# Four transfers and one group of products take another place in the order of a gated attention and ReGLU kernel (forward and gradients)

## The chip, the cores and the metric

The kernel runs on one core of one Trainium2 chip. The time is that of the device for one execution, in microseconds (us). Before the change the median of three runs is 909.66 us, from 908.64 to 911.75 us.

The core has five engines, each with its own queue of instructions that it takes in order: PE (TensorE, the matrix products), DVE (VectorE), ACT (ScalarE), POOL (GpSimd) and SP (SyncE, here used only to issue transfers). Transfers (DMAs) are issued from SP, from ACT and, for a few, from POOL.

## The reference

The kernel computes the output of a small network and all its gradients for one given gradient of the output. With S = 2048 tokens, D = 512, F = 1376, 32 heads of width 16 and a window of 256:

```
g   = sigmoid((x * gate_w).sum(-1))            # one gate per token
a   = attention(x @ wqkv, causal, window 256) @ wo     # O @ wo
b   = (relu(x @ W_gate) * (x @ W_up)) @ W_down # h @ W_down
out = g * a + (1 - g) * b
outputs: out, d/dx, d/dwqkv, d/dwo, d/dW_gate, d/dW_up, d/dW_down, d/dgate_w
```

All inputs and outputs are bf16. In the kernel, h is the inner product of the second branch, dg and du are the gradients of its two factors, O is the attention's output ahead of `wo`, and dq, dk, dv are the gradients of the attention's projections.

## The kernel before

The work has four stages. Every stage is written out by hand: the code emits each engine's instructions in the order in which they run.

**Stage 1, the second branch (lines 448 to 511, up to about 250 us).** A loop over n makes 44 steps: 11 blocks of 128 rows of F (`fc`) by 4 blocks of 512 tokens (`tg`). `at(lag)` is the step that began lag rounds earlier. In each round PE makes the gate product (`gate`, ACT then makes `rg`), the product `up` (DVE makes `upm`, POOL makes `hT`), the product `dh` of the step two rounds back (ACT makes `dh_sb`, DVE makes dg and POOL makes du, both in one tile `dgu`), and from round 6 on the weight gradients of the step six rounds back (`weights`, lines 402 to 436). The three products of the round share three PSUM buffers in turn (tag `mm`), so that the gate product of a round needs the buffer that ACT empties with `rg` of the round before. SP turns h and dg with du by transfers that transpose (`turn_h`, `turn_dgu`). ACT issues the stores of h, dg and du to scratch memory in HBM (`keep`, line 398): h of the step three rounds back, dg and du of the step four rounds back.

**Stage 2, the attention and its gradients (lines 512 to 974, about 250 to 705 us).** A loop over 360 units of 128 by 512 scores. Near its end, while the last units are still in work, it issues first loads for the next stage: `ev` holds actions for a later round, and line 897 puts the load of the first h (block 0, `load_h(0)`) two rounds behind unit row 13 and the second (`load_h(1)`) two rounds behind unit row 15. The stage spills its results (dq, dk, dv and O by rows) to the scratch `dqkvo_d`.

**Stage 3a, the first pass over the tokens (lines 976 to 1031, about 705 to 768 us).** Eight groups `g` of two blocks of 128 tokens. Before it starts, `load_a(0)` and `load_a(1)` load grad_out (`go_g`) and O (`o_t`) of groups 0 and 1; then come weights that are turned (`W_rest`), and the last of the gradients of `wqkv` (`S2["grads"]`, four products `wps` that DVE and ACT empty into `ws` in turn and that ACT stores). Per token block PE makes `bps` = h @ W_down (11 matmuls, ACT empties it into `b_all`) and adds four matmuls to `dwo` with `da_r`, which DVE makes from `go_g`.

**Stage 3b, the second pass (lines 1033 to 1110, about 768 us to the end).** The same groups. `load_b(g)` brings three operands: the rows of `dqkvo_d` turned by one transposing transfer (`T_g`, in the trace `turned`), `dgT_g` and `duT_g`. `load_b(0)` is issued in the first pass, ahead of block 12. Per block PE makes `aps` = O @ wo (4 matmuls, reads `T_g`), then `dx_in` (22 matmuls into `dxps`, from `dgT_g` and `duT_g`), then the part of the next block's sums `dgw` and `dx_qkv` (12 matmuls into `dxps`, reads `T_g`). From `aps` ACT, DVE and POOL make the output rows and the scalar `dz`, which `dx_out` needs to empty `dxps`.

**What else sets the order.** Each transfer that SP or ACT issues signals one of eight semaphores, taken in turn over both engines in the order of the program, and it waits until the transfer that had this semaphore before, eight issues earlier, has landed. While it waits, everything behind it on its engine waits too.

Of the kernel before, what the change touches and what calls it, by code (L numbers as in the profile page):

```python
# [12 lines left out]
F32 = mybir.dt.float32  # L13
# [9 lines left out]
def kernel(  # L23
# [20 lines left out]
    nc = tc.nc  # L44
    P = 128
# [4 lines left out]
    S, D = x_d.shape  # L50
# [7 lines left out]
    FC = (F + P - 1) // P  # L58
    TGW = min(512, S)
    NTG = S // TGW  # L60
    TPG = TGW // P
# [21 lines left out]
    dgT_d = dram.tile([F, S], BF, name="dgT_d")  # L83
    duT_d = dram.tile([F, S], BF, name="duT_d")
    dqkvo_d = dram.tile([S, 4 * D], BF, name="dqkvo_d")
# [112 lines left out]
    with ExitStack() as p1, tc.manual_schedule():  # L198
# [199 lines left out]
        def keep(k, *pairs):  # L398
            for dst, src in pairs:
                nc.scalar.dma_start(dst[k.fsl, k.ts], src)  # L400
# [47 lines left out]
        for n in range(N1 + 8):  # L448
            at = lambda lag: steps[n - lag] if 0 <= n - lag < N1 else None
            if at(0):  # L450
                gate(at(0))
                if 0 < n < NTG:
                    gate_col(n)
                if n == 2:
                    turn_wd0()
                if n + 1 < NTG:
                    turn_x(n + 1)
                if n == 0:
                    turn_gw()
                up(at(0))  # L460
                if n == 0:
                    gate_col(n)
                if n < NTG:
                    db_rows(n)
                if at(0).tg == 0 and at(0).fc > 0:
                    turn_wd(at(0).fc)
            if 1 <= n <= NTG:
                turn_db(n - 1)
            if at(2):
                dh(at(2))  # L470
            if at(1):
                turn_h(at(1))
            if at(3):
                keep(at(3), (hT_d, at(3).hT[:]))
            if at(4):
                turn_dgu(at(4))
                keep(at(4), (dgT_d, at(4).dgT), (duT_d, at(4).duT))
            if at(6):
                f = weights(at(6))
                if f is not None:  # L480
                    stores[n + 1] = f
            if n in stores:
                stores.pop(n)()
            t = n - DA0
            if t % 2 == 1 and 0 <= t // 2 < NT:
                make_da(t // 2)
            if t % 2 == 0 and 0 < t // 2 <= NT:
                turn_da(t // 2 - 1)
            if t == 2:
                nc.vector.reduce_sum(par[:, 0:1], par4[:], axis=AX.X)  # L490
                nc.vector.tensor_scalar(par[:, 1:2], par[:, 0:1], -1.0, 1.0, op0=ALU.mult, op1=ALU.add)
            if n == NTG + 1:
                nc.scalar.activation(tiny[:], tiny[:], ACT.Exp)
            if t in (NT + 3, 2 * NT + 1):
                i = (t - NT - 3) // (NT - 2)
                nc.gpsimd.memset(zt[i][:, 0, :, :, :], 0.0)
                nc.vector.memset(zt[i][:, 1, :, :, :], 0.0)
            if n == N1 - 2:
                first = project_parts(*groups[0])
            for _ in range({N1 + 1: 2, N1 + 2: 0}.get(n, 1)):  # L500
                if first:
                    first.pop(0)()
            if n == N1 + 2:
                second = project_parts(*groups[1])
            if n in (N1 + 2, N1 + 3, N1 + 4):
                second.pop(0)()
            z = n - DA0 - NT - 2
            if z == 0:
                load_w(0)
            if z % 4 == 3 and 0 < z // 4 + 1 < DC:  # L510
                load_w(z // 4 + 1)

    p3 = ctx
    if True:
# [55 lines left out]
        W6 = {}  # L570
# [91 lines left out]
        for c in range(DC):  # L662
            for j in range(NT):
                kbs = [k for k in (j - 1, j, j - 2) if k >= 0]
                for half in range(2):
                    order = kbs if half or len(kbs) < 3 else [kbs[0], kbs[2], kbs[1]]
                    for ki, kb in enumerate(order):
                        u = Unit()
# [129 lines left out]
        def load_f(dst, src_d, gsl):  # L798
            nc.sync.dma_start(dst[:, :nfull, :], src_d[0:nfull * P, gsl].rearrange("(fc p) s -> p fc s", p=P))
            if nfull < FC:  # L800
                nc.sync.dma_start(dst[:, nfull, :], src_d[F - P:F, gsl])

        def tokens(g):
            return slice(g * GT * P, (g + 1) * GT * P)

        def load_h(g):
            flat = wq.tile([P, 2, TPG, NP, P], BF, tag=f"z{g % 2}", name=f"h{g % 2}")[:].rearrange("p w t h q -> p (w t h q)")
            S2[f"h{g}"] = flat[:, 0:FC * GT * P].rearrange("p (c s) -> p c s", c=FC)
            load_f(S2[f"h{g}"], hT_d, tokens(g))
# [4 lines left out]
            return go_g  # L814

        def load_a(g):
            if g > 1:
                load_h(g)
            S2[f"go{g}"] = load_go(g)
            o_v = dqkvo_d[tokens(g), :].rearrange("(t p) (c a n) -> p t c a n", p=P, c=DC, a=4)  # L820
            for tl in range(GT):
                t = g * GT + tl
                o_t = pjA.tile([P, DC, P], BF, tag=("K0", "K1", "V0", "V1")[t % 4], name="o_t")
                nc.sync.dma_start(o_t[:], o_v[:, tl, :, 3, :])
                S2[f"o{t}"] = o_t

        def load_b(g):
            if g % 2 == 0:
                S2["T"] = st.tile([P, NT, 4, P], BF, tag="rows_st", name="turned")[:].rearrange("p t a n -> p (t a n)")
            n1 = 4 * DC * GT * P  # L830
            T_g = S2["T"][:, g % 2 * n1:(g % 2 + 1) * n1].rearrange("p (c s) -> p c s", c=4 * DC)
            nc.sync.dma_start_transpose(out=T_g, in_=dqkvo_d[tokens(g), :])
            dgT_g = S2["g6"].tile([P, FC, GT * P], BF, tag="dgT_g", name="dgT_g")
            load_f(dgT_g, dgT_d, tokens(g))
            duT_g = S2["g6"].tile([P, FC, GT * P], BF, tag="duT_g", name="duT_g")
            load_f(duT_g, duT_d, tokens(g))
            return T_g, dgT_g, duT_g

        with tc.manual_schedule():
            ev = {}  # L840
# [6 lines left out]
            n = 0  # L847
# [28 lines left out]
            while n <= NU + LAG or ev or cdq or bgq:  # L876
                now = ev.pop(n, [])
                u = units[n] if n < NU else None
                if u is not None:
                    gi = u.c * NTG + u.j // TPG  # L880
                    if u.first and u.j == 0:
                        sts[u.c] = st.tile([P, NT, 4, P], BF, tag="rows_st", name="rows_st")
                    if u.first and u.j % TPG == 0:
                        if gi + 1 < len(groups):
                            prq = project_parts(*groups[gi + 1]) if gi else second
                            due = n + sum(2 * min(3, j + 1) for j in range(u.j, u.j + TPG)) - 3
                            if gi + 2 == len(groups):
                                due -= 10
                    if u.first and u.j == TPG and ends:
                        copies.append(ends.pop(0))  # L890
                    if u.first and u.j == 1 and u.c > 0:
                        ready = grad_parts(u.c - 1)
                    if u.first and u.j == TPG - 1 and u.c > 0:
                        bgq += ready
                    front(u)
                    if u.last and gi + 1 == len(groups) and u.j % TPG in (1, 3):
                        ev.setdefault(n + 2, []).append(("dma", lambda i=(u.j % TPG) // 2: load_h(i)))
                for eng, f in now:
                    if eng == "pool":
                        f()  # L900
# [10 lines left out]
                w = units[n - LAG] if LAG <= n < NU + LAG else None  # L911
# [66 lines left out]
            S2["t6"] = ctx.enter_context(tc.tile_pool(name="t6", bufs=2))  # L978
            while late:
                late.pop(0)()  # L980
            load_a(0)
            load_a(1)
            for _ in range(4):
                W_rest.pop(0)()
# [7 lines left out]
    with ExitStack() as p56:  # L992
        x_r5 = x_r

        with ExitStack() as p6, tc.manual_schedule():
# [10 lines left out]
            for t in range(NT):  # L1006
                g, tl = t // GT, t % GT
# [25 lines left out]
            for g in range(NG):  # L1033
# [5 lines left out]
                for tl in range(GT):  # L1039
                    t = g * GT + tl  # L1040
                    tsl = slice(t * P, (t + 1) * P)
                    lsl = slice(tl * P, (tl + 1) * P)
                    aps = ps6r.tile([P, D], F32, tag=f"r{t % 2}", name="aps")
                    for c in range(DC):
                        nc.tensor.matmul(aps[:], lhsT=T_g[:, 4 * c + 3, lsl], rhs=W6[("wo", c)],
# [16 lines left out]
                    nc.vector.tensor_tensor(out=dz[:, 2:3], in0=dz[:, 0:1], in1=dz[:, 1:2], op=ALU.mult)  # L1062
                    dz_bf = t6.tile([P, 1], BF, tag="dz_bf", bufs=3)
                    nc.vector.tensor_copy(dz_bf[:], dz[:, 2:3])
                    def dx_in(to, cols):
                        for src, wt in ((dgT_g, "Wg"), (duT_g, "Wu")):
                            for fc in range(FC):
                                nc.tensor.matmul(to, lhsT=src[:, fc, lsl], rhs=W6[(wt, fc)][:, cols],  # L1068
                                                 start=(fc == 0 and wt == "Wg"), stop=False)

                    def dx_qkv(to, cols, cc):
                        nc.tensor.matmul(to, lhsT=T_g[:, 4 * (cc % DC) + cc // DC, lsl], rhs=W6[("wqkv", cc)][:, cols],  # L1072
                                         start=False, stop=(cc == C3 - 1))
# [4 lines left out]
                                                       op0=ALU.mult, op1=ALU.add)  # L1078
                        (nc.sync if t == NT - 1 else nc.gpsimd).dma_start(dx_d[tsl, cols], dx_sb[:, cols])

                    dxps = ps6.tile([P, D], F32, tag=f"w{t % 2}", name="dxps")
                    cols = slice(0, D)
                    if t == NT - 1:
                        low, cols = slice(0, D // 2), slice(D // 2, D)
                        low_ps = ps6r.tile([P, D], F32, tag="r2", name="low_ps")
# [1 line left out]
                        for cc in range(C3):  # L1087
                            dx_qkv(low_ps[:, low], low, cc)
                        dx_out(low_ps[:, low], low)
                    dx_in(dxps[:, cols], cols)  # L1090
                    def add_dgw(t_, dz_):
                        for c in range(DC):
                            nc.tensor.matmul(dgw_ps[:, c:c + 1], lhsT=x_r5[:, t_, c * P:(c + 1) * P], rhs=dz_[:],
# [47 lines left out]
```

## Time and profile before

| | us |
|---|---|
| median of three runs | 909.66 |
| the profiled execution | 907.26 |
| its span, first to last instruction | 905.5 |
| PE busy in the span | 889.5 |
| PE busy, 0 to 36 us | 32.60 of 36.00 |
| PE busy, 36 to 250 us | 214.00 of 214.00 |
| PE busy, 250 to 700 us | 442.93 of 450.00 |
| PE busy, 700 to 722 us | 20.36 of 22.00 |
| PE busy, 722 to 768 us | 46.00 of 46.00 |
| PE busy, 768 us to the end | 133.59 of 137.50 |

The granted clock of TensorE is 1.00 in all of these. A line of the timeline gives the start in us from the start of the span, the time taken, the engine (a q behind it marks an issue or a wait of its sequencer), the line of the code, the operation, what it writes and reads, how many instructions the row merges, and in brackets the engine's idle time before it with what ended it. Matmuls overlap: a row shows each with 0.38 us or so for 512 columns, but in an unbroken stream their starts are about 0.2155 us apart (22 matmuls of `dx_in` in 4.74 us between 778.29 and 783.03). An idle time in brackets therefore starts only at the modelled end of the last matmul, some 0.16 us later than the next could have started.

### The profile page before, as it was taken

The numbers are of one execution on the slowest core, as the hardware profiler recorded it, in microseconds if no ns is written. First come the engines' busy times: TensorE is split into PE (matmuls) and PEld (weight loads), VectorE is DVE, ScalarE is ACT, GpSimd is POOL, SyncE is SP. The second block draws the span as 40 slices with busy tenths as digits, with TensorE's granted clock in tenths as the row PEclk, the third lists the DMA queues.
The fourth block names the chain that finished last, engine by engine and source line by source line (L and its number), as shares of the span: only waits on it lengthen the run. The fifth ranks groups of instructions, "written<-read, shape, count | busy, mean of one in ns | idle before, by whom it ended". The sixth has DMA issues, their size and how long they took to land.

```text
span 905.5 us, 25962 instructions
## 1 busy us (share of the span) xinstructions
PE 889.5 (98%) x10607; PEld 560.2 (62%) x10607; DVE 511.1 (56%) x946; ACT 445.5 (49%) x787; POOL 492.8 (54%) x937
## 2 busy tenths in 40 slices
PE   9999999999989999999999999999999999999998
PEld 5565655655657777677776677766677544444445
DVE  4433334434368887678886788877786101333343
ACT  6422232222278778667776677766787112111111
POOL 4544545545267778767777567876787100222232
PEclk9999999999999999999999999999999999999999
DMA  9998989999799999999999989999999899998940
GB/s 301 204 193 185 198 181 210 215 216 216 180 138 159 190 185 197 185 171 156 175 187 183 184 161 183 187 193 183 192 219 190 222 243 228 275 255 218 189 134 30
DMA packets 520984, 174.57 MB, mean 193 GB/s; under 512 B 446817, under 2 KB 519745, under 8 KB 520865
## 3 DMA queue, kind: packets, MB, share of 16 engines
q1 hardware_dynamic: 498624, 150.62, 89.6%
q10 hardware_dynamic: 20608, 17.70, 7.5%
q0 software_dynamic: 1632, 4.59, 1.5%
q8 instruction: 83, 1.36, 0.6%
q14 instruction: 37, 0.30, 0.1%
HBM read 34.37 MB, written 36.24 MB: 78 GB/s over the span
## 4 chain that ended last, share of the span: by engine, by line
PE 85%; DMA 4%; DVE 4%; ACT 2%; POOL 2%; SPq 2%; issue 1%; ACTq 0%; POOLq 0%; DVEq 0%
PE dxps L1068 8%; PE wps L412 8%; PE ST L687 7%; PE dPT L710 7%; PE pt L753 5%; PE dxps L1072 4%; PE dps L414 4%; PE pp L133 4%; PE dhps L363 4%; PE ups L363 4%; PE CD L541 4%; PE gps L363 4%; PE BA L724 4%; PE wps L641 4%; PE bps L1023 3%; PE BA L726 2%
## 5 line engine op out<-in xcount | busy, mean ns | idle before, releaser
L687 PE MATMUL ST<-z,K 128*128 128x512 bf16 x360 | 135.9, 378 | 3.3 <-ACT PPd L696 1.2
L710 PE MATMUL dPT<-z,V 128*128 128x512 bf16 x360 | 136.0, 378 | 1.8 <-DVE Pd L715 0.5
L698 POOL TENSOR_SCALAR_AFFINE_SELECT PPd<-PPd 128x512 bf16<-128x512 bf16 x128 | 81.3, 636 | 80.1 <-ACT PPd L696 80.0
L377 POOL TENSOR_TENSOR hT<-rg,upm 128x512 bf16<-128x512 bf16 x44 | 51.0, 1160 | 113.8 <-DVE upm L375 97.5
L412 PE MATMUL wps<-dgu_r,x_r 128*128 128x256 bf16 (+1 forms) x704 | 103.9, 270 | 0.0
L715 DVE TENSOR_TENSOR PPd<-PPd,dPT 128x512 bf16<-128x512 bf16 x128 | 86.9, 680 | 19.9 <-PE dPT L710 12.3
L701 POOL TENSOR_SCALAR_AFFINE_SELECT Pu<-Pu 128x512 bf16<-128x512 bf16 x112 | 72.0, 643 | 35.1 <-ACT Pu L696 34.0
L696 ACT ACTIVATE PPd<-ST 128x512 bf16<-128x512 f32 x128 | 77.0, 603 | 23.6 <-PE ST L687 18.8
L715 DVE TENSOR_TENSOR Pd<-Pu,dPT 128x512 bf16<-128x512 bf16 x112 | 76.4, 682 | 21.0 <-PE dPT L710 10.6
L412 PEld LDWEIGHTS <-x_r 128*128 128x128 bf16 x704 | 68.4, 98 | 30.9 <-issue 0.2
L696 ACT ACTIVATE Pu<-ST 128x512 bf16<-128x512 f32 x112 | 67.4, 602 | 37.2 <-PE ST L687 37.1
L715 DVE TENSOR_TENSOR PPm<-PPm,dPT 128x512 bf16<-128x512 bf16 x120 | 80.1, 667 | 7.1 <-PE dPT L710 6.1
L696 ACT ACTIVATE PPm<-ST 128x512 bf16<-128x512 f32 x120 | 72.5, 604 | 16.7 <-PE ST L687 16.2
L375 DVE SCALAR_TENSOR_TENSOR upm<-rg,ups 128x512 bf16<-128x512 bf16 x44 | 30.2, 685 | 81.8 <-ACT rg L369 43.1
L369 ACT ACTIVATE rg<-gps 128x512 bf16<-128x512 f32 x44 | 26.3, 597 | 89.0 <-PE gps L363 47.4
L414 PE MATMUL dps<-db_r,h_r 128*128 128x512 bf16 x176 | 66.8, 379 | 0.0
L1048 ACT COPY a_sb<-aps 128x512 f32<-128x512 f32 x16 | 9.4, 585 | 108.0 <-issue 99.8
L72 ACT COPY p<-pt 128x1024 bf16<-128x1024 bf16 x59 | 60.1, 1019 | 4.2
L387 POOL TENSOR_TENSOR dgu<-dh_sb,rg 128x512 bf16<-128x512 bf16 x44 | 58.0, 1318 | 5.3 <-ACT dh_sb L383 5.3
L386 DVE TENSOR_TENSOR dgu<-dh_sb,upm 128x512 bf16<-128x512 bf16 x44 | 34.5, 784 | 29.8 <-ACT dh_sb L383 26.1
L641 PE MATMUL wps<-rows_st,x_r 128*128 128x384 bf16 x256 | 50.3, 325 | 0.0
L133 PE MATMUL pp<-x,p 128*128 128x512 bf16 x192 | 49.0, 378 | 0.0
(178 smaller groups left out, 2323.2 us busy)
## 6 DMA issues: line engine op xcount, KB each, us to landing
dqkvo_d<-rows_st SPq DMA_DIRECT2D x15, 512.0 KB, 4.3
hT_d<-hT ACTq DMA_DIRECT2D x44, 128.0 KB, 2.5
dgT_d<-dgu ACTq DMA_DIRECT2D x44, 128.0 KB, 2.9
duT_d<-dgu ACTq DMA_DIRECT2D x44, 128.0 KB, 3.0
h<-hT_d SPq DMA_DIRECT2D x8, 640.0 KB, 4.9
dgT_g<-dgT_d SPq DMA_DIRECT2D x8, 640.0 KB, 5.2
duT_g<-duT_d SPq DMA_DIRECT2D x8, 640.0 KB, 6.5
go_g<-in_grad_out_dram SPq DMA_DIRECT2D x16, 256.0 KB, 4.7
```

The lines of the kernel that those rows point to most:

```text
L133: nc.tensor.matmul(pp[:], lhsT=w_p[c][:, cd, which * P:(which + 1) * P], rhs=x_T[tg][:, cd, :], start=(cd == 0), stop=(cd == DC - 1))
L363: nc.tensor.matmul(out[:], lhsT=w(c), rhs=x(c), start=(c == 0), stop=(c == DC - 1))
L412: nc.tensor.matmul(acc["w"][:, c, 0:2 * nw], lhsT=x_r[:, t, c * P:(c + 1) * P], rhs=k.dgu_r[:, :, i, s0:P], start=(go_ and c % 2 == 0), st ...
L414: nc.tensor.matmul(acc["d"][:], lhsT=k.h_r[:, i, :], rhs=db_r[:, t, :], start=go_, stop=no_)
L641: nc.tensor.matmul(wps[:], lhsT=x_r[:, t, part * P:(part + 1) * P], rhs=sts[c][:, t, 0:3, :], start=first and t == t0, stop=last and t == ...
L687: nc.tensor.matmul(ST[:], lhsT=KTt[:, ksl], rhs=z[:, 0, :, jl, :], start=True, stop=True)
L696: nc.scalar.activation(u.Pu[:], ST[:], ACT.Exp)
L698: nc.gpsimd.affine_select(out=u.Pu[:], in_=u.Pu[:], compare_op=ALU.is_ge, fill=0.0, base=0, pattern=[[0, HH], [1, P]], channel_multiplier=-1)
L701: nc.gpsimd.affine_select(out=u.Pu[:], in_=u.Pu[:], compare_op=ALU.is_ge, fill=0.0, base=-1, pattern=[[0, HH], [-1, P]], channel_multiplier=1)
L710: nc.tensor.matmul(u.dPT[:], lhsT=VTt[:, ksl], rhs=z[:, 1, :, jl, :], start=True, stop=True)
L715: nc.vector.tensor_tensor(out=u.Pd[:], in0=u.Pu[:], in1=u.dPT[:], op=ALU.mult)
L1068: nc.tensor.matmul(to, lhsT=src[:, fc, lsl], rhs=W6[(wt, fc)][:, cols], start=(fc == 0 and wt == "Wg"), stop=False)
```

## The change

1. `keep` for dg and du moves from four rounds back to five: ACT issues the two stores one round later.
2. `load_a` loads its h itself for all groups but the first. Behind unit row 15 the loop of stage 2 now issues `load_a(0)` (the first grad_out and the first two blocks of O) in the place of `load_h(1)`; behind the loop `load_a(1)` issues the second h ahead of the second grad_out and O.
3. `load_b(0)` issues the loads of `dgT_g` and `duT_g` ahead of the transposing transfer; all other groups keep the order.
4. In block 0 of the second pass the 22 matmuls of `dx_in` go ahead of `aps`. Their sum `dxps` then lies in the PSUM buffer `r2`, which `bps` of block 14 used, and not in `w0`.

```diff
-                keep(at(4), (dgT_d, at(4).dgT), (duT_d, at(4).duT))
+            if at(5):
+                keep(at(5), (dgT_d, at(5).dgT), (duT_d, at(5).duT))
...
         def load_a(g):
-            if g > 1:
+            if g > 0:
                 load_h(g)
             S2[f"go{g}"] = load_go(g)
...
-            nc.sync.dma_start_transpose(out=T_g, in_=dqkvo_d[tokens(g), :])
+            if g > 0:
+                nc.sync.dma_start_transpose(out=T_g, in_=dqkvo_d[tokens(g), :])
             dgT_g = S2["g6"].tile([P, FC, GT * P], BF, tag="dgT_g", name="dgT_g")
             load_f(dgT_g, dgT_d, tokens(g))
             duT_g = S2["g6"].tile([P, FC, GT * P], BF, tag="duT_g", name="duT_g")
             load_f(duT_g, duT_d, tokens(g))
+            if g == 0:
+                nc.sync.dma_start_transpose(out=T_g, in_=dqkvo_d[tokens(g), :])
             return T_g, dgT_g, duT_g
...
-                        ev.setdefault(n + 2, []).append(("dma", lambda i=(u.j % TPG) // 2: load_h(i)))
+                        ev.setdefault(n + 2, []).append(("dma", (lambda: load_a(0)) if u.j % TPG == 3 else lambda: load_h(0)))
...
-            load_a(0)
             load_a(1)
...
+                    dxps = (ps6 if t else ps6r).tile([P, D], F32, tag=f"w{t % 2}" if t else "r2", name="dxps")
+                    cols = slice(0, D)
+                    if t == 0:
+                        dx_in(dxps[:, cols], cols)
                     aps = ps6r.tile([P, D], F32, tag=f"r{t % 2}", name="aps")
...
-                    dxps = ps6.tile([P, D], F32, tag=f"w{t % 2}", name="dxps")
-                    cols = slice(0, D)
...
-                    dx_in(dxps[:, cols], cols)
+                    if t > 0:
+                        dx_in(dxps[:, cols], cols)
```

`dx_in` itself is moved up unchanged.

More of the change, by code (lines that the diff above doesn't have):

```diff
@@ L1042, with dx_in @@
                     lsl = slice(tl * P, (tl + 1) * P)
+                    def dx_in(to, cols):
+                        for src, wt in ((dgT_g, "Wg"), (duT_g, "Wu")):
+                            for fc in range(FC):
+                                nc.tensor.matmul(to, lhsT=src[:, fc, lsl], rhs=W6[(wt, fc)][:, cols],
+                                                 start=(fc == 0 and wt == "Wg"), stop=False)
+                    dxps = (ps6 if t else ps6r).tile([P, D], F32, tag=f"w{t % 2}" if t else "r2", name="dxps")
+                    cols = slice(0, D)
+                    if t == 0:
+                        dx_in(dxps[:, cols], cols)
                     aps = ps6r.tile([P, D], F32, tag=f"r{t % 2}", name="aps")
@@ L1064 @@
                     nc.vector.tensor_copy(dz_bf[:], dz[:, 2:3])
[L1065 to L1069, printed above, removed]
                     def dx_qkv(to, cols, cc):
```

## The prediction

> **What bounds the kernel now.** The page comes first: PE is busy for 889.5 of 905.5 us, so only what PE loses can be won. The list of PE's waits says where; here are the three that the change can touch, all of them single events:
>
> ```profile
> PE dwo L1027 <- ACT ws L72: 1.2, 1, 1.2
> PE gps L363 <- ACT rg L369: 1.1, 1, 1.1
> PE dxps L1068 <- DMA dgT_g<-dgT_d: 0.8, 1, 0.8
> ```
>
> The table of stretches says what a gain in stage 1 is worth and what a harm there would have to do first: from 36 to 250 us PE has no idle time at all.
>
> ```profile
> 36.00:250.00 214.00, 214.00 (x1346) 130.25 (x1345) 85.30 (x127) 58.97 (x103) 99.46 (x82) 1.00 0.94 197
> ```
>
> Then the timeline around each wait. Round 5 of stage 1, PE and ACT:
>
> ```profile
> 28.30 1.03 PE L363 MATMUL dhps<-db_T,WdT 128*128 128x512 bf16 x4
> 30.39 1.02 PE L363 MATMUL gps<-x,Wg_sb 128*128 128x512 bf16 x4 [1.07 <-ACT rg L369]
> ...
> 28.22 0.35 ACTq L400 DMA_DIRECT2D hT_d<-hT  x1
> 28.61 0.46 ACTq L400 DMA_DIRECT2D dgT_d<-dgu  x1
> 29.32 0.33 ACTq L400 DMA_DIRECT2D duT_d<-dgu  x1
> 29.75 0.60 ACT L369 ACTIVATE rg<-gps 128x512 bf16<-128x512 f32 x1 [2.34 <-PE dhps L363]
> ```
>
> The input of this rg was there since 27.6, but ACT stood at three stores, each waiting for the transfer eight issues earlier. The chain of waits shows such a wait: du's next store starts at 33.45, just as a turned h lands (28.97 + 4.46 = 33.43):
>
> ```profile
> 28.97 4.46 DMA h_r<-hT
> 33.43 0.02 issue
> 33.45 0.33 ACTq L400
> ```
>
> The seam to the first pass, SP, DVE, ACT and PE:
>
> ```profile
> 705.49 0.53 SPq L799 DMA_DIRECT2D h<-hT_d  x1
> ...
> 707.23 0.50 SPq L813 DMA_DIRECT2D go_g<-in_grad_out_dram  x1
> 707.78 3.48 SPq L824 DMA_DIRECT2D o_t<-dqkvo_d  x2
> ...
> 714.51 0.62 DVE L1020 TENSOR_SCALAR da_r<-go_g,g_all 128x512 bf16<-128x512 bf16 x2 [1.83 <-DMA go_g<-in_grad_out_dram]
> 715.04 1.02 DVE L74 CAST ws<-wps 128x384 bf16<-128x384 f32 x2
> ...
> 715.74 0.65 ACTq L633 DMA_DIRECT2D out_dram<-ws  x1
> ...
> 718.74 1.02 PE L1027 MATMUL dwo<-da_r,o_t 128*128 128x512 bf16 x4 [1.19 <-ACT ws L72]
> ```
>
> grad_out lands late; DVE has da_r ahead of the finished products ws; ACT's stores wait for DVE; the last ws leaves PSUM at 718.69 and dwo can start. The seam to the second pass, SP and PE:
>
> ```profile
> 759.67 4.75 SPq L832 DMA_TRANSPOSE turned<-dqkvo_d  x1
> 764.88 0.41 SPq L799 DMA_DIRECT2D dgT_g<-dgT_d  x1
> ...
> 769.96 1.04 PE L1068 MATMUL dxps<-x,dgT_g 128*128 128x512 bf16 x4 [0.77 <-DMA dgT_g<-dgT_d]
> ```
>
> The transposing transfer holds SP for 4.75 us, so dgT_g is issued at 764.88 and lands 5.0 us later.
>
> **The change part by part.** I count by starts of matmuls, 0.2155 us apart.
>
> *A, the stores a round later.* It adds and removes no instruction. The products dhps let PE go on at 28.30 + 4 x 0.2155 = 29.16; the gate product came at 30.39, 1.23 lost. In round 7 the same once more: the last weight product starts at 35.38, the gate product at 35.84 instead of 35.60, 0.24 lost, because rg ran only at 35.21. After the change ACT goes from the h store (ends 28.57) to rg (0.60), done at 29.2, the gate product at 29.25: 0.09 stays. In the next round ACT has dh_sb until 29.93, three stores of 0.33 to 0.46 until about 31.2, the table load (1.28) and its small activation (0.20) and rg until 33.3; the next gate product is due at 29.25 + 12 x 0.2155 + 4 x 0.65 = 34.4. So A gains 1.23 + 0.24 - 0.09 = 1.4. Lower end 0: if the du store in its new place waits like the one at 33.45, rg again ends at 35.8 and the next gate product stands where it stood. Upper end 1.47. I take 1.4, since the transfer eight issues ahead of the new place is by my count an h turned at 25.61, which had landed by the h store of 29.85. From 36 us on the same stores sit one round later in the same place among the same five issues a round: 0, covered by ACT's waits (rg waits 3 us for its product in a round such as 108 to 114 us). At the end of stage 1 the last two stores slide behind 242.5 us, where ACT is idle until 249.65: 0.
>
> *B, grad_out and O ahead of the second h.* Three SP issues go to 705.49, past two issues of h1 and one spill. They wait for nothing new: the K buffers that take O were last read by scores at 697.6. Behind them on SP stand the spill (first read by group 4, some 25 us later), h1 (wanted by the third bps at 722.8) and the second grad_out (wanted at 719.8, at its old place since the sum of issues ahead of it is the same): 0. grad_out lands 4.7 to 7.3 us after its issue (the rows at 711.36 and 707.23), at 710.2 to 712.8. DVE is free for da_r at 712.7; the first of the four products is done at about 713.15; ws is out by 714.0 and not 715.6. From the first store to dwo ACT took 718.74 - 715.74 = 3.0 us, so dwo could start at 717.15, and bps lets PE go at 716.74 + 3 x 0.2155 = 717.39: the whole 1.35 could go. But the first store's semaphore was that of O's first load; after the change it is that of h1, which is now issued late. h1 is issued at 707.7 if O's loads take 0.6 each (row 712.08) and at 710.0 if they take the 3.48 of before, and lands 4.8 (alone, 748.07) to 6.7 us later (the row at 705.49): 712.5 to 716.7. Since the same transfers together were in by 715.3 before (O's second load, 709.26 + 6.0), I take 715.1: store at 715.1, dwo at 718.1, B gains 0.65. Ends: 1.35, and 718.74 - 719.7 = -0.95.
>
> *C, turned rows behind dg and du, dx_in ahead of aps.* No instruction more. dgT_g is issued at 759.67 and lands at 764.7, duT_g (four issues to 761.9) at about 767.2, by the 2.5 us between the two before; dx_in starts at 768.16, straight behind dwo. Turned rows: issue from 762.1, landing 7.0 to 9.6 us later (this row, and the one at 771.20), 769.1 to 771.7; aps wants them at 768.16 + 22 x 0.2155 = 772.9: covered. Gain: 769.96 - 769.02 for the wait, and the 0.13 by which dx_in then ran over 4.74, together 1.05. Lower end 0.65: duT_g's second issue may take 2.17 as before, then the rows land at 773.3. Upper end 1.07. What is late next: aps ends 4.7 us later, so dz of block 0 comes at about 780.3; dx_out waits for it on DVE, and o_sb of block 1 behind that until 781, against 779.7. dz of block 1 then comes near 786 and is wanted at 790.5; the buffer r2 is wanted again in block 15: 0.
>
> The Trainium skill (TensorE: Matmul & The Clock Gate, Back-to-back issue gap) puts a sustained stream of weight loads and 512-column matmuls at 131 ns each. The trace has 215.5, so it decides; by the page's figure, as an estimate, the 22 matmuls would take 2.9 us, aps would want its rows at 771.1, could wait 0.6 for them, and C would be 0.45.
>
> **Sum.** 1.4 + 0.65 + 1.05 = 3.1 us, all of it on PE, which has no slack behind any of the three. From the profiled execution that is 907.26 - 3.1 = 904.2 (span 902.4). The median is 2.4 above that execution, so 909.66 - 3.1 = 906.6, 0.34% less. A difference under 0.3% (2.7 us) I count as the same, about what a measurement of this kernel can tell from none.
>
> **Rivals.**
> *R1, a waiting issue takes the gain back.* The rule of eight moves with the order: ACT's first product store waits for h1 up to 716.7 (B = -0.95), or du's first store waits to 33.4 (A = 0). Alone, the first leaves 1.4 - 0.95 + 1.05 = 1.5, 908.2; the second 1.7, 908.0. Both end within 0.3%. For it: h1 took 6.7 us in the crowd at 705 against 4.9 alone. Against: h1's crowd ends at 715.3. The Trainium skill (DMA: Bandwidth & Descriptors, Issuing engines are not separate DMA queues) has all DMAs run on the same 16 engines and interleave, whoever issues them; by that rule h1 pays for what was put ahead of it, as its 6.7 us agree.
> *R2, slower: the stores block ACT in the ten rounds that close a block of F.* There the four SP issues of results and weights turn the eight semaphores within one round; a late dg or du store holds up the emptying of wps, which has one buffer. At 114 us DVE empties it until 115.13 and PE wants it at 116.42, 1.3 us of room; ACT's longest wait for such a store is 3.0 us, so up to 1.7 x 10 = 17 us, 923. It decides from a mean wait of 1.3 + (3.1 + 2.7) / 10 = 1.9 us. Against: the order within a round stays, the data are ready a round earlier, and PE's idle time is nil there today.
> *R3, nothing moves:* another wait stands just behind each of the three, 909.7. Against: the starts worked out above find none.
>
> **How the numbers follow.** Forecast, 0.57, faster; R1 0.26 and R3 0.03, same; R2 and the like 0.14, slower. The terms' ends give 3.9 (905.8) and, with all three low, -0.3 (910.0); the runs before lie 1.0 below to 2.1 above their median, so the range is 904.8 to 910.4, which leaves out R2 and little else.
>
> **What would show it.** Right: no idle time on PE ahead of the gate product near 30 us; in the first pass dwo at most 0.7 us behind bps; in the second dx_in straight behind dwo, and aps without a wait. Wrong: ACT standing at a store in round 6, the first ws store starting with h1's landing after 715.7, or aps waiting for turned rows.

## The result and the profile after

The changed kernel takes 907.39 us (median of 14 runs, 904.91 to 909.89); the kernel before 909.51 (14 runs, 908.14 to 911.75). The ratio is 0.9975, 95% interval 0.9964 to 0.9986: 0.25% or 2.3 us less, with 1.3 to 3.3 us inside the interval. That is a gain; the median lies below the 3.1 us forecast, which the interval still holds, and by the forecast's own bound of 0.3% it counts as no change. Measured again later in the study it was 906.42 against 908.26, ratio 0.998 (0.9968 to 0.9991).

The list of PE's waits of the changed kernel (total us, how often, longest):

```profile
PE ptx L289 <- DMA x_r<-in_A_x_dram: 1.6, 1, 1.6
...
PE CD L542 <- DMA p2m<-PPm: 1.1, 1, 1.1
PE dwo L1030 <- ACT ws L72: 1.0, 1, 1.0
```

Two of the three waits that the change aimed at are gone: the gate product's on rg and dx_in's on dgT_g. The third, dwo on ws, is still there at nearly its old size. Two waits that the change does not touch were longer in this execution: the one for the second half of x (0.55 before) and the one for p2m (0.53 before).

The two profiled executions have the same span of 905.5 us although the medians differ. That of the changed kernel lost 2.09 us within the first 12 us, and 0.64 more ahead of the first pass with the longer wait for p2m; and that of the kernel before (907.26) was shorter than all 14 of its runs. Stretches of 2 us at the start (busy us of PE, PEld, DVE, ACT and POOL; then the granted clock), the first line from before, the others from after:

```profile
8.00:10.00 2.00, 2.00 (x36) 1.53 (x34) 0.97 (x3) 1.42 (x2) 0.00 (x0) 1.00 1.09 362
...
6.00:8.00 2.00, 1.35 (x11) 0.78 (x12) 0.42 (x1) 0.59 (x1) 0.00 (x0) 0.85 1.09 331
8.00:10.00 2.00, 2.00 (x15) 1.45 (x13) 0.08 (x1) 0.60 (x1) 0.00 (x0) 0.50 1.09 364
10.00:12.00 2.00, 2.00 (x29) 1.49 (x28) 0.89 (x3) 1.01 (x1) 0.00 (x0) 0.80 1.09 350
```

PE is busy all through the row of 8 to 10 us but starts 15 matmuls there, at a clock of 0.50; the kernel before had 36, at 1.00. The second gate product starts at 12.00 us and not at 9.90. The change does not come into play before 28 us, so its effect has to be read from there on, as shifts of starts against before. The first place, rounds 6 and 7 of stage 1, PE and ACT; the first line is the second gate product before:

```profile
35.84 1.02 PE L363 MATMUL gps<-x,Wg_sb 128*128 128x512 bf16 x4
...
30.39 1.03 PE L363 MATMUL dhps<-db_T,WdT 128*128 128x512 bf16 x4
31.26 1.03 PE L363 MATMUL gps<-x,Wg_sb 128*128 128x512 bf16 x4
36.46 1.03 PE L363 MATMUL gps<-x,Wg_sb 128*128 128x512 bf16 x4
...
29.79 0.60 ACT L369 ACTIVATE rg<-gps 128x512 bf16<-128x512 f32 x1 [0.28 <-PE gps L363]
31.83 0.47 ACTq L400 DMA_DIRECT2D dgT_d<-dgu  x1
32.34 0.47 ACTq L400 DMA_DIRECT2D duT_d<-dgu  x1
32.84 1.28 ACT L494 ACT_TABLE_LOAD   x1 [0.80 <-issue]
34.25 0.58 ACT L369 ACTIVATE rg<-gps 128x512 bf16<-128x512 f32 x1
```

dhps is 2.09 us later than before (30.39 against 28.30), the next gate product only 0.87 (31.26 against 30.39), the one after it 0.62 (36.46 against 35.84). So this place won 1.22 + 0.25 = 1.47 us. rg no longer stands behind three stores; the two stores run a round later, 0.47 us each, and neither waits for an older transfer.

The second place, the seam to the first pass (PE before, then DVE, ACT and PE after):

```profile
716.74 0.81 PE L1023 MATMUL bps<-p,h 128*128 128x512 bf16 x3
...
713.85 0.58 DVE L1023 TENSOR_SCALAR da_r<-go_g,g_all 128x512 bf16<-128x512 bf16 x2
714.52 0.56 DVE L74 CAST ws<-wps 128x384 bf16<-128x384 f32 x1
...
716.68 0.65 ACTq L634 DMA_DIRECT2D out_dram<-ws  x1
...
718.00 0.81 PE L1026 MATMUL bps<-p,h 128*128 128x512 bf16 x3
719.77 1.02 PE L1030 MATMUL dwo<-da_r,o_t 128*128 128x512 bf16 x4 [0.96 <-ACT ws L72]
```

da_r has no idle time ahead of it any more, and the first ws is ready at 714.52 + 0.56 = 715.08. But ACT's store of it starts only at 716.68. The second h says why. SP issues it in two pieces, at 710.33 and 710.82; this is the second, and the answer for the tile gives its time from issue to landing:

```profile
L802 SPq DMA_DIRECT2D h<-hT_d x1: 1242/1242/1242, 710.8 to 710.8; - x1
...
DMA to landing us min/median/max: 5.8/5.8/5.8
```

710.8 + 5.8 = 716.6: the store starts as this piece lands. By the order of issue the transfer eight ahead of the first store is the first piece, and the second piece is eight ahead of the second store. The landing of the first piece is not on record; where those of both are, it lands 0.2 us ahead of the second (712.23 and 712.44 in the kernel before). The profile puts ACT's idle time here down to the second grad_out, but that one, issued at 712.16, landed 5.3 us later, at 717.4, when the store had gone. dwo then starts 1.03 us later than before, while bps ahead of it was 1.26 later (718.00 against 716.74): 0.23 us won.

The third place, the seam to the second pass, first before, then after:

```profile
767.30 1.03 PE L1027 MATMUL dwo<-da_r,o_t 128*128 128x512 bf16 x4
...
777.42 0.60 PE L1045 MATMUL aps<-wo_z,turned 128*128 128x512 bf16 x2
...
768.33 1.03 PE L1030 MATMUL dwo<-da_r,o_t 128*128 128x512 bf16 x4
769.19 1.03 PE L1049 MATMUL dxps<-x,dgT_g 128*128 128x512 bf16 x4
...
773.94 0.59 PE L1058 MATMUL aps<-wo_z,turned 128*128 128x512 bf16 x2
...
777.39 0.59 PE L1058 MATMUL aps<-wo_z,turned 128*128 128x512 bf16 x2
```

dx_in starts 4 x 0.2155 us behind dwo, aps follows without a wait, and aps of block 1, at 777.42 before, is at 777.39: the 1.03 us by which dwo was late and 0.03 more are made up, 1.06. Between these two traces the change is worth 1.47 + 0.23 + 1.06 = 2.76 us, inside the measured 1.3 to 3.3.

### The profile page after: what moved, and what is told of

It is laid out like the page before. It is cut to its first block, busy times and chain, and to the rows that moved or that the text cites. A ratio compares the mean times of both kernels' runs of the same rounds, so it can differ in the third digit from the quotient of the medians.

```text
span 905.5 us, 25948 instructions
## 1 busy us (share of the span) xinstructions
PE 889.8 (98%) x10607; PEld 561.2 (62%) x10607; DVE 510.8 (56%) x946; ACT 445.6 (49%) x787; POOL 493.9 (55%) x937
## 4 chain that ended last, share of the span: by engine, by line
PE 86%; DVE 5%; POOL 2%; ACT 2%; DMA 2%; issue 1%; SPq 1%; ACTq 0%; POOLq 0%; DVEq 0%
PE wps L412 8%; PE dxps L1049 8%; PE ST L688 7%; PE dPT L711 7%; PE pt L754 5%; PE dxps L1079 4%; PE gps L363 4%; PE dhps L363 4%; PE dps L414 4%; PE ups L363 4%; PE bps L1026 4%; PE pp L133 4%; PE BA L725 4%; PE CD L542 4%; PE wps L642 4%; PE BA L727 2%
```

## Experiments

**The parts one by one.** Three kernels, each with one part of the change. First the stores alone:

```diff
-                keep(at(4), (dgT_d, at(4).dgT), (duT_d, at(4).duT))
+            if at(5):
+                keep(at(5), (dgT_d, at(5).dgT), (duT_d, at(5).duT))
```

> The kernel before with part 1 of the change alone: dg and du are stored one round later. Theory (the stores blocked ACT ahead of rg in rounds 5 and 6): the gate product near 30 us follows the product dhps without a wait, and the next one follows the weight products; together 1.5 us less on PE, counted from the first product after the start, and about 1.2 to 1.5 us (0.13 to 0.17%) in the time. Rival (the wait reappears one round later at the du store): the gate product of round 7 stands where it stood against the start of stage 1, and the time is unchanged. A second rival, that the late start of stage 1 seen in the profile after comes from the moved stores, expects such a late start here and in no run of the kernel before.

Measured: 906.89 against 908.62 us, ratio 0.9985 (0.9973 to 0.9998), 0.15% or 1.4 us. Counted by starts 0.2155 us apart, the first gate product is 0.05 us late in its trace (29.39, with dhps at 28.48) and the second still 0.41 (35.03, with the last weight product at 34.41). Here the rival shows in part: the store of dg in its new place starts only at 31.99, as the turned dg and du issued eight issues earlier, at 27.63, land 4.3 us later. The start of the kernel is not slow: the clock is 1.00, the wait for x 0.6 us.

Then grad_out and O ahead of the second h, alone:

```diff
-            if g > 1:
+            if g > 0:
                 load_h(g)
...
-                        ev.setdefault(n + 2, []).append(("dma", lambda i=(u.j % TPG) // 2: load_h(i)))
+                        ev.setdefault(n + 2, []).append(("dma", (lambda: load_a(0)) if u.j % TPG == 3 else lambda: load_h(0)))
...
-            load_a(0)
```

> The kernel before with part 2 alone: the first grad_out and O ahead of the second h. Theory (ACT's first store of the finished products waits for the transfer eight issues earlier, now the second h): da_r and ws come 1 us earlier on DVE, yet the first store starts only when the second h has landed, and the wait of PE ahead of dwo falls from 1.2 us only to about 0.9 to 1.0; the time moves by 0.2 to 0.3 us, too little to measure. Rival (the landing of grad_out is all that holds the store): the wait is gone and the time falls by 1.2 to 1.35 us, 0.14%.

Measured: 908.39, ratio 0.9995 (0.9984 to 1.0005): nothing that can be told from no change. Its trace at the seam:

```profile
715.29 0.56 DVE L74 CAST ws<-wps 128x384 bf16<-128x384 f32 x1
...
716.76 0.65 ACTq L633 DMA_DIRECT2D out_dram<-ws  x1
...
719.82 1.02 PE L1026 MATMUL dwo<-da_r,o_t 128*128 128x512 bf16 x4 [0.23 <-ACT ws L72]
```

ws is ready at 715.85 and the store starts 0.91 later, right behind the landing of the second h at 716.71 (issued at 711.77, 4.9 us). So the mechanism is the same as in the whole change. By the starts PE loses 0.40 us ahead of dwo, 0.95 less than before. The wait of dwo is only 0.23 because PE came to bps at 717.04, 0.77 later than in the changed kernel, while the store started at nearly the same time. How long dwo waits depends on how PE and SP stand to each other in an execution; the kernel that follows, which leaves this place as it was, had no wait there at all, PE having waited 2.1 us for p2m ahead of it.

Last the second seam, parts 3 and 4 of the change (their lines as in the diff above):

> The kernel before with parts 3 and 4: turned rows behind dg and du, and the first block's dg and du products ahead of aps. Theory: no wait of PE between the first and the second pass, 1.05 us less (0.12%). Rival (the turned rows land after the 22 products): aps waits for them, by up to 0.6 us, and the gain is 0.45 us.

Measured: 907.65, ratio 0.9987 (0.9974 to 1.0), 0.13% or 1.2 us. dx_in starts straight behind dwo (769.53 and 770.39) and aps without a wait (775.14). The three parts together give 0.15 + 0.05 + 0.13 = 0.33%; the whole measured 0.25 and 0.20%. The intervals are as wide as that difference, so it is not evidence that the parts hinder each other.

**Do parts 3 and 4 need each other?** The turned rows behind dg and du, but aps still first:

```diff
-            nc.sync.dma_start_transpose(out=T_g, in_=dqkvo_d[tokens(g), :])
+            if g > 0:
+                nc.sync.dma_start_transpose(out=T_g, in_=dqkvo_d[tokens(g), :])
             ...
+            if g == 0:
+                nc.sync.dma_start_transpose(out=T_g, in_=dqkvo_d[tokens(g), :])
```

> The kernel before with part 3 alone: the turned rows behind dg and du, but aps still ahead of the 22 products. Theory (the turned rows land 7 to 10 us after an issue that is now 2 to 5 us later): aps waits for them, by 3 to 5 us, and the products behind it don't wait; PE loses 2 to 4 us against the kernel before at the seam between the passes. Rival (the turned rows were not what the load of dg waited for, they land in time anyway): no wait ahead of aps, and 0.8 to 1 us less at the seam.

Measured in a single execution: 916.93 against 909.37 us. And dx_in ahead of aps, with the transposing transfer still first:

```diff
...
+                    if t == 0:
+                        dx_in(dxps[:, cols], cols)
                     aps = ps6r.tile([P, D], F32, tag=f"r{t % 2}", name="aps")
...
-                    dx_in(dxps[:, cols], cols)
+                    if t > 0:
+                        dx_in(dxps[:, cols], cols)
```

> The kernel before with part 4 alone: the 22 products ahead of aps, the turned rows still issued first. Theory: dg lands at the same time as before, so PE waits for it where aps stood, 0.86 us longer than before (1.6 us or so in the list of waits), and aps follows later without a wait; the seam costs the same as before to within 0.2 us, since PE reaches the end of block 0 at the same time. Rival (the order of the products alone wins the 1.05 us): the wait is gone.

Measured in a single execution: 912.43 against 909.37. At the seam each half alone costs more than its wait. The timeline of the first of the two:

```profile
775.96 1.03 PE L1048 MATMUL aps<-wo_z,turned 128*128 128x512 bf16 x2 [3.55 <-DMA turned<-dqkvo_d]
...
777.64 1.91 PE L1071 MATMUL dxps<-x,dgT_g 128*128 128x512 bf16 x4
...
782.11 1.03 PE L1071 MATMUL dxps<-d,duT_g 128*128 128x512 bf16 x4
```

and of the second:

```profile
772.69 1.08 PE L1046 MATMUL dxps<-x,dgT_g 128*128 128x512 bf16 x4 [2.83 <-DMA dgT_g<-dgT_d]
773.56 1.91 PE L1046 MATMUL dxps<-d,dgT_g 128*128 128x512 bf16 x4
...
779.13 0.59 PE L1055 MATMUL aps<-wo_z,turned 128*128 128x512 bf16 x2
```

The figure to look at is the second of a row that merges four matmuls (x4): 1.03 us as elsewhere, 1.91 behind the wait (for two, x2, 0.59 and 1.03). The stretches of the first of the two kernels show the granted clock, third number from the end:

```profile
774.00:776.00 2.00, 0.04 (x1) 0.05 (x2) 0.00 (x0) 0.00 (x0) 0.00 (x0) 0.76 1.14 258
776.00:778.00 2.00, 2.00 (x5) 0.69 (x6) 0.00 (x0) 0.12 (x1) 0.00 (x0) 0.50 1.00 307
778.00:780.00 2.00, 2.00 (x6) 0.76 (x5) 0.79 (x2) 1.15 (x2) 0.00 (x0) 0.50 1.07 181
780.00:782.00 2.00, 1.78 (x5) 0.70 (x5) 0.57 (x1) 0.00 (x0) 1.44 (x2) 0.53 1.24 274
782.00:784.00 2.00, 2.00 (x11) 0.88 (x9) 1.07 (x4) 0.00 (x0) 0.28 (x1) 1.00 1.06 260
```

These two long waits cost twice: the idle time, and then matmuls at half speed. From the end of dwo to the first dx_qkv of block 0 the kernel before needs 774.83 - 768.16 = 6.67 us. Here it is 784.48 - 772.24 = 12.24 in the first, 5.57 more, and 780.00 - 769.69 = 10.31 in the second, 3.64 more. The waits, 3.72 and 3.00 us from the end of dwo, less the 1.06 that the kernel before loses here, explain 2.66 and 1.94 of that; the other 2.9 and 1.7 are the slow matmuls. The rest of the first kernel's 7.6 us need not come from the edit: its trace is already 4.25 us behind the one before at the first bps (719.26 against 715.01), ahead of anything that the edit moves.

**The store that waits for the second h.** If the transfer eight issues earlier is the cause, issuing the second h behind the second grad_out and O makes that transfer an earlier one, the second grad_out:

```diff
         def load_a(g):
-            if g > 0:
+            if g > 1:
                 load_h(g)
             ...
+            if g == 1:
+                load_h(g)
```

> The changed kernel, with the second h issued behind the second grad_out and O. The eight semaphores then give ACT's four product stores those of the second grad_out, the third and fourth O and, for the last store alone, the second h. Theory (eight issues back): the first store starts when ws is out, about 1.5 us earlier than after the change; PE's wait ahead of dwo is gone or under 0.2 us; with the changed kernel's other gains the time is 0.35% under the kernel before and about 1.1 us under the changed one. Rival (the store waits for the crowd of transfers as such, or for DVE): the wait ahead of dwo stays at 0.9 to 1.0 us. The price to look for: the third bps waits for the second h.

Measured: 905.45, ratio to the kernel before 0.9967 (0.9955 to 0.9978). Its trace:

```profile
712.35 0.56 DVE L74 CAST ws<-wps 128x384 bf16<-128x384 f32 x1
713.06 0.65 ACTq L634 DMA_DIRECT2D out_dram<-ws  x1
...
715.83 0.81 PE L1028 MATMUL bps<-p,h 128*128 128x512 bf16 x3
716.55 1.02 PE L1032 MATMUL dwo<-da_r,o_t 128*128 128x512 bf16 x4
```

The store follows ws (712.91) at once, although the second h lands only at 715.55, and dwo stands behind bps without a wait in the list (by the starts it loses 0.08). The second h is late for nobody: the third bps is at 720.65.

The same cause can be taken away at its other end: the changed kernel with the four product stores issued from POOL, so that ACT issues none of them.

```diff
-                return lambda: (nc.scalar if tail else nc.sync).dma_start(to, ws[:])
+                return lambda: (nc.gpsimd if tail else nc.sync).dma_start(to, ws[:])
```

> The changed kernel with the four product stores issued from POOL instead of ACT; the second h stays ahead of the second grad_out and O. Theory (ACT stood at a store that waited for the second h): ACT empties its two products as soon as they are done, the wait ahead of dwo is gone although the second h lands as late as in the changed kernel, and the time is 0.8 to 1.2 us under the changed kernel's (0.33% under the kernel before). Rival (the crowd of transfers, not the semaphore, held it): the wait ahead of dwo stays at 0.2 to 1.0 us and the time is the changed kernel's. Price to look for: POOL's stores take longer to issue (0.96 us in the trace).

Measured: 906.07 against 909.37, ratio 0.995 (0.9929 to 0.9971). ACT empties the products with no regard to the second h, which lands at 718.16:

```profile
716.23 0.56 DVE L74 CAST ws<-wps 128x384 bf16<-128x384 f32 x1
716.92 0.48 ACT L72 CAST ws<-wps 128x384 bf16<-128x384 f32 x1 [1.12 <-DMA go_g<-in_grad_out_dram]
...
718.17 0.48 ACT L72 CAST ws<-wps 128x384 bf16<-128x384 f32 x1 [0.78 <-PE wps L642]
```

(Here too the profile names the second grad_out, which landed only at 718.84.) dwo follows bps without a wait. That dwo's wait is gone would not prove it by itself, since without any such edit it is also gone in the changed kernel's second trace (further down, the change as it is):

```profile
715.21 0.65 ACTq L634 DMA_DIRECT2D out_dram<-ws  x1
...
717.97 0.81 PE L1026 MATMUL bps<-p,h 128*128 128x512 bf16 x3
718.64 1.02 PE L1030 MATMUL dwo<-da_r,o_t 128*128 128x512 bf16 x4
```

What shows it is the start of the store. With the change's order of loads it starts 0.03 to 0.05 us behind the landing of the second h's second piece in the three traces where ws was ready before that, and 0.15 behind ws in this one, where the second h had landed at 714.97 and ws was ready at 715.06. With the second h last it starts 0.15 behind ws in all four traces, while the second h is still 2.5 to 3.4 us from landing; and with the stores on POOL ACT does not wait. In the three traces where the store waited, the second grad_out landed 0.8 us behind its start, so it was not that. That the second h held the store is shown.

**The start.** Five matmuls of no use into a free PSUM buffer, between the two halves of the first turned block of x, on top of the second h issued last:

```diff
+                if half == 0:
+                    for _ in range(5):
+                        nc.tensor.matmul(wps0[:], lhsT=warm[:, 0:P], rhs=warm[:], start=True, stop=True)
```

> The kernel with the second h last, and five more matmuls without use on PE between the two halves of x at the start, where the profile after had PE idle for 1.6 us and then the granted clock at 0.5 to 0.85 until 12 us. Theory (an idle PE loses the clock): no execution with a mean granted clock under 1.000, the slowest executions 2 us faster, the median 0 to 0.5 us under the kernel without them. Rival (the low clock has another cause): such executions stay at one in seven or so, and the median is the same or up to 0.3 us worse for the added matmuls.

Measured: 906.09, ratio 0.9956 (0.9939 to 0.9973), the mean granted clock 1.000 in all 7 runs. But the same kernel without the fill had 1.000 in all of its 9 runs on another chip too, so this does not settle what the fill is worth.

**All four side by side.** Therefore the changed kernel as it is, with the fill, with the second h last, and with both, on one chip with the same runs of the kernel before (908.26, 25 runs):

> The changed kernel once more, as the base for the other three. Ratio to the kernel before about 0.9972, between 0.996 and 0.9985: the trace's sum 1.47 + 0.23 + 1.06 = 2.8 us of 909, less what chance takes at the start, where about a third of the executions have a granted clock under 1.000 and are then some 2 us longer. By the rival, that the change itself brings the slow start, its share of executions with a clock of 0.998 or less is well above that of the kernel before, and the ratio 0.998 or more.

> The changed kernel with five matmuls of no use between the two halves of the first turned block of x, so that PE does not stand idle while the second half of x comes late. Theory (the idle time of over a microsecond lowers the granted clock, and that costs about 2 us): clock 1.000 in all executions, median 0.3 to 1.0 us below the changed kernel. Rival (what costs is the late x alone, and the clock only marks it): the median as the changed kernel's within 0.3 us, or above by up to 0.5 for the matmuls added.

> The changed kernel with the second h issued behind the second grad_out and O. Theory (the first product store waits for the second h, eight issues earlier): dwo starts straight behind bps, 1.0 us below the changed kernel, between 0.6 and 1.4. Rival (the wait ahead of dwo has slack behind it): within 0.3 us of the changed kernel.

> Both edits together. Theory: the two add up, 1.3 to 2.0 us below the changed kernel, ratio to the kernel before about 0.9955, clock 1.000 in all executions. Rival: no better than the second h behind alone, within 0.3 us of it.

| kernel | median us | ratio to before, 95% interval | runs | runs with a mean clock of 0.998 |
|---|---|---|---|---|
| the change | 906.42 | 0.998 (0.9968 to 0.9991) | 11 | 0 |
| with the fill | 905.79 | 0.9976 (0.9966 to 0.9987) | 12 | 1 |
| second h last | 905.45 | 0.9968 (0.9957 to 0.9979) | 6 | 1 |
| both | 905.43 | 0.9967 (0.9955 to 0.9979) | 6 | 0 |

The second h last is 0.97 us faster than the change, as expected (1.0). The intervals of the two overlap, but of all measurements here the four with this edit (0.9967, 0.9956, 0.9968, 0.9967) lie below the three with the change's own order of loads and its stores on ACT (0.9975, 0.998, 0.9976). It is faster than the kernel before, and probably than the changed kernel, but that last step of 1 us lies within the noise. Both edits together were expected to be 1.3 to 2.0 us below the change and are 0.99, no better than the second h last alone. In their trace dwo still waits 0.18 us: ACT's last ws stands behind a store whose issue took 1.35 us there and 0.66 in the changed kernel; why is not shown. The fill is not shown to be worth anything: with it the medians are 0.63 and 0.02 us lower, and one run had the low clock all the same. Nor is it shown that the change brings a mean clock of 0.998 or less: none of these 11 runs has it and 5 of the first 14 had, with a median of 907.46 against 907.32 in the other 9; of the kernel before it is 4 of 32, 3 of 12 and 1 of 25 on three chips. And the mean does not tell where the clock fell: in the profiled execution with parts 3 and 4 alone it was at 692 us.

The trace of the change with the fill is of use in another way. It has the change's order of loads, and PE reaches its third group of bps matmuls at 716.83, where the kernel before has 716.74:

```profile
715.04 0.64 ACTq L637 DMA_DIRECT2D out_dram<-ws  x1
...
716.83 0.81 PE L1029 MATMUL bps<-p,h 128*128 128x512 bf16 x3
718.17 1.02 PE L1033 MATMUL dwo<-da_r,o_t 128*128 128x512 bf16 x4 [0.53 <-ACT ws L72]
```

Here the second h landed at 715.01 and the store left at 715.04, and dwo waits 0.53 us: 718.74 + 0.09 - 718.17 = 0.66 won in place of 0.23.

## Why the prediction came out as it did

**A, the stores: right.** 1.4 forecast, 1.47 in the trace (its upper end), 1.4 in the kernel with this part alone. The 0.09 us that I left ahead of the gate product was not there; the kernel with part 1 alone still loses 0.46 us at the two gate products. The loss itself is not the same in every execution: the five traces with the stores in their old place lose 1.5, 1.3, 1.6, 0.0 and 0.8 us here, the nine with the new place 0.0 to 0.5.

**C, the second seam: right, by its steps.** 1.05 forecast (its two terms, 0.94 and 0.13, add up to 1.07), 1.06 in the trace, 1.2 alone. The three traces without parts 3 and 4 lose 1.1 to 1.9 us here, the nine with both 0.01. dgT_g was issued at 760.88 and landed 5.4 us later, ahead of dx_in (forecast 764.7 from 759.67, 5.0 later); the turned rows were issued at 764.90 and landed at 772.64, 1.30 ahead of aps. The forecast that they would be issued from 762.1 missed, since duT_g's second issue did take 2.33: set back by the 1.21 us by which SP was later, they went out at 763.69, the case of the lower end. But they landed 7.74 us later and not the 9.6 reckoned there, so aps did not wait. That was within the range taken, and some luck. By the estimate from the Trainium skill's figure (TensorE: Matmul & The Clock Gate, Back-to-back issue gap) aps would have waited 0.6; the trace, with dx_in's 22 matmuls in 773.94 - 769.19 = 4.75 us or 0.216 each, does not agree.

**B, the first seam: the mechanism right, one term mis-sized.** The prediction had the first store wait for the second h. What failed is the step "I take 715.1" for its landing. Set back by PE's 1.26 us, the store started at 715.42, 0.32 later than taken, and dwo followed it by 3.09 and not 3.0 us: 0.41 together, 0.65 - 0.41 = 0.24, against 0.23 measured. The transfer itself was not slow: its second piece took 5.8 us from issue to landing, and 6.4 in the kernel before, from 706.06 to 712.44. Its issue was late. SP came to the first of these loads at 707.27, not at the 705.49 from which I counted, because the transposing transfer ahead of it held SP for longer, and PE was late by less. So I took a time on SP and a time on PE from one execution as if their distance were fixed. Over executions it is not: against the loss of 1.35 us before, the change's order of loads gave 0.23 in one trace, 0.66, what I forecast, in another, 0.95 with part 2 alone and 1.33 in the changed kernel's second trace, where the second h was in before ws was ready. Nor is the loss before a constant: the five traces with the old order lose 1.35, 1.01, 0, 1.19 and 1.20 us, the four with the change's 1.12, 0.40, 0.02 and 0.69. So neither the 0.23 nor a hit on 0.65 would say much; that part 2 gains anything in the time is not shown (0.9984 to 1.0005 alone).

**The sum and the median.** 3.1 forecast, 2.76 between the two traces, 2.3 and 1.8 by the ratios of two comparisons, of which the first interval holds 3.1 and the second, to 2.9, does not. Of the difference between forecast and traces, B is 0.42. That one pair of traces comes so near is luck in part, since A and B vary by over a microsecond; on the mean of all traces with the old and the new order the three places lose 0.95, 0.4 and 1.35 us less, 2.7 together. What remains is within the intervals. The upper end of the range does not follow from its terms: 910.0 + 2.1 is 912.1 and not 910.4.

**The rivals.** R1 took part of B, not all of it: its mechanism decided at the first store, and its -0.95 did not come. Its other half, a store that waits in its new place, came for dg in the kernel with part 1 alone (0.41 us) and not in the trace of the change. The Trainium skill (DMA: Bandwidth & Descriptors, Issuing engines are not separate DMA queues) has all transfers interleave on the same 16 engines; what I drew from it, that the second h pays for what is put ahead of it, is not borne out by 5.8 us against 6.4. R2 did not come. PE waits for wst at wps for 0.3 to 1.1 us in total in seven of the nine traces with part 1 (0.5 with part 1 alone, none in the first trace of the change), and for 1.1 to 1.9 in three of the five without it (1.9 with part 3 alone), far from 17. R3 did not come either: no new wait stands behind the three, as the list of waits shows.

**My expectations on the experiments** missed in several: dx_in ahead of aps alone was to cost about what it gained, and cost 3.6 us at the seam, and the turned rows alone were to cost 2 to 4 and cost 5.6, since I had not reckoned with the clock; dwo's wait in the kernel with part 2 alone was 0.23 and not near 1; the fill did not keep the clock at 1.000 in all runs; and the two edits together did not add up.

## What to carry to other kernels

When a transfer is moved, count not only when its own data come but which later issue now waits for it; here a store inherited a wait from a load that nobody needed for another 7 us, and with that load issued last the median was 1 us lower, in intervals that overlap. A new order of loads and the new order of the products that read them belong together: each half alone cost 3.6 to 5.6 us at the seam, in one trace each, and both together won 1. And a distance between two queues that is read off one execution is a sample: where the gain hangs on it, look for the wait whose removal makes it not matter.

## What was not expected of the hardware

Short waits of PE can lower its granted clock, and the time at half clock comes in one length. From the stretches (the missing share of the clock, doubled, times 2 us) it is 0.6 + 2.0 + 0.8 = 3.4 us at the start of the changed kernel's trace, behind a wait of 1.63 us, 3.4 with the stores on POOL (wait 1.65), 3.4 from 692 us on in the kernel with parts 3 and 4 alone (wait 1.28 at 691.02; 0.58 and 0.57 from 692 to 696), 3.4 at the seam where dx_in waited 2.83, and 6.8, twice that, where aps waited 3.55. After all waits up to 1.27, and after 1.33 (turned rows alone, at 688.16), 1.50 (the changed kernel's second trace, at the start) and 1.57 (part 1 alone, at 686.33), it stayed at 1.00. So the length of the wait alone does not decide; what does is not shown. One start fits neither: behind a wait of 1.26 us four matmuls took 1.87 us (turned rows alone), with stretches that show 1.00; that stays open too. The Trainium skill (TensorE: Matmul & The Clock Gate, What's actually happening) has the clock fall to half after at least one idle window of about 3.4 us and come back after one such window of work. Half and 3.4 us agree with the traces; that waits of 1.28 and 1.63 us were enough does not. Where the clock falls for 3.4 us, PE loses up to 1.7 us beyond the wait, as at the seam with dx_in alone, and removing such a wait can win more than its idle time.
